# An mLSTM and MLP kernel: late gates on 128 partitions, and less work turned by TensorE

## The chip, the cores and the metric

The kernel runs on one core of one Trainium2 chip. A core has TensorE (matrix products), VectorE, ScalarE, GpSimd and SyncE, each with an instruction queue of its own that it works off in order, and 16 DMA engines. The metric is the device time of one execution in microseconds.

## What is computed

An mLSTM layer (4 batches, 8 heads, 768 time steps, head size 40) is followed by a gated MLP on its 3072 rows of 320 features. Per batch and head, over time t:

```python
m_new = np.maximum(f[t] + m, i[t])
f_stab, i_stab, m = np.exp(f[t] + m - m_new), np.exp(i[t] - m_new), m_new
C = f_stab * C + i_stab * outer(v[t], k[t])
n = f_stab * n + i_stab * k[t]
y[t] = sigmoid(o[t]) * (C @ q[t]) / max(abs(n @ q[t]), 1)
# then, for all rows x of y: 
h = x @ w_in            # 320 -> 2048
out = (h * sigmoid(h)) @ w_out
```

## The kernel before

Time is cut into 12 pieces of 64 steps. A *unit* is one piece for two of the four batches, so there are 24; unit n has piece n // 2. A unit multiplies scores (keys with queries), weighs them by the gates (tile D), adds up its own values ("near", from D) and the values of the running state ("far", from qt, the queries times lq), divides, and gives x: 128 rows of 320 features. It also adds to the state Cm.

Three units make a *step* of the MLP, so there are 8. `Step.mm1` (line 849) makes ph, the hidden layer, for one of 16 feature chunks of 128, `Step.act` (856 to 880) the gate product g, `Step.mm2` (901) the output. TensorE alternates between the first product of chunk fc and the second of chunk fc - 2, and the loop over steps j and chunks fc (from `for j in range(NSTEP)`) puts between them what the next three units need. In step 0 the units 3, 4 and 5 are done at chunks 5, 9 and 12 (`PLACES`): `block` (scores of the next unit, near and far values, state), `close` (weighing, line 576, and norm), `level`, `scale`, `carry` (the state, lines 747 and 757). The PSUM pool `psH` has two buffers, which ph and half of a unit's state use in turn.

The order on every engine is the order in which the code is written; no scheduler changes it. The table `FILL`, chunk by chunk, says what else is done in step 0: `wmake(n)` makes the next n weight parts (two ScalarE passes, lines 280 and 281, then VectorE, 282, into wi, wo or wtc) and issues the load of a later part on SP's queue; `halve` splits a wtc part into wh (303, 305). So weights, gates and units share VectorE and ScalarE in step 0. In the steps 1 to 7 the weights are there.

The **gates** come from two inputs of 32 rows (batch and head) by 768 columns (time), side by side in the tile `home` as f, i, m, LF and a pattern. `gates(lo, hi)` (167 to 185) scans m, then forms the exponents and scans LF within each piece, all on 32 partitions. Columns 0 to 255 are done early; `late` does 256 to 767 in two halves of 256 in the chunks 3 to 12. `spread` writes LF of two pieces to DRAM (LFd), from where units load it as D and lq, and turns the gate sums i into aT (time on the partitions) with three TensorE transposes (line 200) and two VectorE copies (207). `spread_far` does the other eight pieces: two VectorE block transposes (228) and ScalarE copies (233).

The **x** of a unit has to be turned, features on the partitions. `xpose` (794) does that with three TensorE transposes into PSUM. For the units in `AROUND` (6 to 23 without 8) `turn_out` instead transposes blocks of 32 on VectorE (766) and stores them to DRAM with four DMAs (768), and `turn_in` loads them back (776). `xput` then splits x into xh (ScalarE, 805) and xl (VectorE, 806).

The **state** of a unit (`state`) is 16 matmuls in 64x64 tiles into two PSUM banks for units from 3 on (line 705), and for units 0 to 2 eight matmuls over all 128 rows into one bank (717), added by `carry` at line 759.

Of the kernel before, what the change touches and what calls it, by code (L numbers as in the profile page):

```python
# [8 lines left out]
F32 = mybir.dt.float32  # L9
# [5 lines left out]
ALU = mybir.AluOpType  # L15
# [4 lines left out]
L = 64  # L20
# [23 lines left out]
def mlstm_mlp_kernel(  # L44
# [6 lines left out]
    fg: bass.AP,  # L51
    w_in: bass.AP,
# [54 lines left out]
    LFd = dr.tile([NC, BH, L], F32, name="LFd")  # L107
# [80 lines left out]
    def spread(lo, hi, eng):  # L188

        c0, c1 = lo // L, hi // L  # L190
        eng.dma_start(
            LFd[c0:c1].rearrange("c r t -> r c t"),
            LF[:, lo:hi].rearrange("r (c t) -> r c t", t=L),
        )
        yield
        pt = psU.tile([128, 512], F32, tag="u", name=f"pt{lo}")

        for c in range(c0 - 1, c1):
            w = slice(c * L, (c + 2 - (c == NC - 1)) * L)
            nc.tensor.transpose(  # L200
                pt[: w.stop - w.start, c * BH : (c + 1) * BH], i_t[:, w], ident[:BH, :BH]
            )
            if (c - c0) % 3 == 1:
                yield
        for k in range(2):
            r = slice(k * L, (k + 1) * L)
            nc.vector.tensor_copy(  # L207
                aT[r, c0:c1, :, :],
                pt[r, (c0 - k) * BH : (c1 - k) * BH].rearrange(
                    "p (c q d h) -> p c q d h", q=NP, d=2, h=H  # L210
                )[:, :, :, k, :],
            )
        yield


    def spread_far(lo, hi, eng):

        c0, c1 = lo // L, hi // L
        eng.dma_start(
            LFd[c0:c1].rearrange("c r t -> r c t"),  # L220
            LF[:, lo:hi].rearrange("r (c t) -> r c t", t=L),
        )
        yield
        n = (c1 - c0) * BH
        src = i_t[:, lo:hi].rearrange("r (c b x) -> r b c x", b=2, x=32)
        at = home[:BH, : 2 * n].rearrange("x (b c r) -> x b c r", b=2, r=BH)
        for b in range(2):
            nc.vector.transpose(at[:, b], src[:, b])
            yield
        for k in range(2):  # L230
            for b in range(2):
                r = k * L + b * 32
                nc.scalar.copy(
                    aT[r : r + 32, c0:c1].rearrange("p c q h -> p (c q) h"),
                    at[:, b].rearrange("x c (q d h) -> x (c q) d h", q=NP, d=2)[:, :, k, :],
                )
            yield
# [132 lines left out]
    for t in Cm:  # L370
        nc.gpsimd.memset(t, 0.0)

# [10 lines left out]
    class Unit:  # L383
# [66 lines left out]
        def load_d(self):  # L450
            n, c, p = self.n, self.c, self.p
            self.Dm = p3.tile([128, H, L], F32, tag="D", name=f"D{n}")
            for k in range(2):
                r = p * 2 * H + k * H
                nc.sync.dma_start(
                    self.Dm[k * L : (k + 1) * L],
                    LFd[c, r : r + H, :].unsqueeze(0).broadcast_to([L, H, L]),
                )
# [28 lines left out]
        def load_q(self):  # L487
            n, c, p = self.n, self.c, self.p
            if c > 0:
                self.lq = p2.tile([128, H, L], F32, tag="lq", name=f"lq{n}")  # L490
                lf = LFd[c, p * 2 * H : (p + 1) * 2 * H, :].rearrange(
# [200 lines left out]
        def state(self):  # L692
# [3 lines left out]
            if n >= UPS:  # L696
                self.pu = [
                    pool_.tile([128, 4, D1], F32, tag=tag, name=f"pu{n}_{tag}")
                    for pool_, tag in ((psU, "u"), (psH, "h"))
# [35 lines left out]
        def carry(self, copy=nc.scalar.copy, steps=(0, 1)):  # L735
# [4 lines left out]
            for a in range(2):  # L740
# [14 lines left out]
                for d in range(2) if n >= UPS else ():  # L755
                    w = v[:, d * 4 : (d + 1) * 4]
                    nc.vector.tensor_tensor(out=w, in0=w, in1=pu[d][r], op=ALU.add)
                if n < UPS:
                    nc.vector.tensor_tensor(out=v, in0=v, in1=pu[r], op=ALU.add)
# [170 lines left out]
    AROUND = set(range(2 * UPS, NU)) - {3 * UPS - 1}  # L930
# [33 lines left out]
    def run(n, it):  # L964
        for _ in range(n):
            next(it, None)
# [31 lines left out]
    for _ in range(2):  # L998
# [4 lines left out]
    near, far = spread(2 * L, 4 * L, nc.gpsimd), spread_far(4 * L, S, nc.gpsimd)  # L1003
    late = [gates(4 * L, 8 * L), gates(8 * L, S)]
# [81 lines left out]
        1: lambda: (wmake(1), u3.expo_act(), u3.keep(), u3.near(), u4.load_qk()),  # L1086
# [13 lines left out]
        3: lambda: (wmake(1), u4.add(), run(1, late[0])),  # L1100
        4: lambda: (wmake(1), u4.exp(), run(1, late[0])),
        5: lambda: wmake(1),
        6: lambda: (halve(4), wmake(2), run(1, late[0])),
        7: lambda: (wmake(1), run(2, late[0])),
        8: lambda: (wmake(1), run(1, late[1])),
        9: lambda: wmake(2),
        10: lambda: (halve(6), wmake(1), run(2, late[1])),
        11: lambda: (wmake(1), run(1, late[1])),
        12: lambda: (wmake(1), run(2, late[1])),
        13: lambda: (wmake(1), run(2, far)),  # L1110
        14: lambda: (units[8].load(), run(1, far)),
        15: lambda: run(3, far),
# [22 lines left out]
    for j in range(NSTEP):  # L1135
        st = steps[j]
        for fc in range(NFC):
# [36 lines left out]
            if 6 in at and at[6].n in AROUND:  # L1174
                at[6].xput(steps[j + 1])
# [9 lines left out]
def _layout(inputs):  # L1185
# [15 lines left out]
    for w, x in enumerate((q, k)):  # L1201
# [21 lines left out]
        "fg": gate(inputs["f_gate"]),  # L1223
        "w_in": bits(w_in[:256]),
# [33 lines left out]
```

## Time and profile before

| | us |
|---|---|
| three runs | 430.94, 431.71, 431.79 |
| their median | 431.71 |
| the profiled execution | 431.02 |
| its span, first to last instruction | 429.2 |

| engine | busy us | share of the span | instructions |
|---|---|---|---|
| TensorE, matmuls | 422.4 | 98% | 5062 |
| TensorE, weight loads | 391.7 | 91% | 5062 |
| VectorE | 288.5 | 67% | 650 |
| ScalarE | 220.6 | 51% | 481 |
| GpSimd | 124.8 | 29% | 135 |

The profile shows one execution of the program. "Start" is us from the span's start. PE is TensorE, PEld its weight loads, DVE VectorE, ACT ScalarE, POOL GpSimd, SP SyncE, SPq its DMA queue. Matmuls overlap, so what one costs is read from the start of the next group. A row such as `th<-ph` names the tile that is written and the one that is read; brackets give the idle time before it and what ended it. The granted clock of TensorE is 1.0 of full speed over the whole span. Step 0 goes from 19.9 to 78.6 us. A row of busy time by stretch gives the stretch and its length, then for PE, PEld, DVE, ACT and POOL the busy us and the number of instructions, the granted clock, the share of time that the 16 DMA engines were busy, and GB/s.

### The profile page before, as it was taken

How to read it: one execution, taken by the hardware profiler on the slowest of the kernel's cores; microseconds unless marked ns; L12 is line 12 of the kernel's file. 1: busy time of each engine (PE TensorE's matmuls, PEld its weight loads, DVE VectorE, ACT ScalarE, POOL GpSimd, SP SyncE). 2: the span in 40 equal slices, each digit the busy share in tenths (PEclk: the TensorE clock that was granted, in tenths of full speed). 3: DMA queues.
4: the chain of work that ended last, by engine and by line, in shares of the span. 5: the costliest groups of instructions: out<-in, count | busy, mean ns of one | idle time of the engine just before them, and what ended most of it. 6: DMA issues, size and time to landing. Idle time of an engine off the chain costs nothing.

```text
span 429.2 us, 12518 instructions
## 1 busy us (share of the span) xinstructions
PE 422.4 (98%) x5062; PEld 391.7 (91%) x5062; DVE 288.5 (67%) x650; ACT 220.6 (51%) x481; POOL 124.8 (29%) x135
## 2 busy tenths in 40 slices
PE   8999999999999999999999999999999999999995
PEld 4767677899999999999999999999999999999995
DVE  5888799877887677467765677566764756443342
ACT  7684866755755454454454644444454543353331
POOL 5734135234234423043412344034320400000000
PEclk9999999999999999999999999999999999999999
DMA  8999696334551775127660575316750231001001
GB/s 272 387 366 311 177 299 165 117 89 141 159 169 21 196 196 155 31 61 189 174 172 2 123 218 139 118 25 179 209 163 22 54 94 20 18 9 39 2 2 46
DMA packets 62650, 57.17 MB, mean 133 GB/s; under 512 B 31440, under 2 KB 49184, under 8 KB 62592
## 3 DMA queue, kind: packets, MB, share of 16 engines
q1 hardware_dynamic: 62288, 55.94, 45.7%
q8 instruction: 40, 0.66, 0.7%
q10 hardware_dynamic: 208, 0.26, 0.2%
q0 software_dynamic: 96, 0.16, 0.1%
q14 instruction: 18, 0.15, 0.1%
HBM read 48.99 MB, written 7.36 MB: 131 GB/s over the span
## 4 chain that ended last, share of the span: by engine, by line
PE 80%; issue 17%; DVE 1%; ACT 1%; POOL 0%; POOLq 0%; ACTq 0%; DVEq 0%
PE ph L849 35%; PE pout L901 33%; PE p L549 3%; PE p L637 2%; PE p L620 2%; PE dummy L999 1%; PE pu_u L705 1%; PE pu_h L705 1%; DVE D L576 0%; PE e L396 0%; PE px L794 0%; PE pu L717 0%; PE po L604 0%; PE p L794 0%; POOL qt L533 0%
## 5 line engine op out<-in xcount | busy, mean ns | idle before, releaser
L856 ACT ACTIVATE th<-ph 128x384 f32<-128x384 f32 x128 | 62.4, 488 | 106.7 <-PE ph L849 106.2
L849 PE MATMUL ph<-xh,wh 128*128 128x384 f32 x336 | 113.8, 339 | 0.0
L849 PE MATMUL ph<-xl,wh 128*128 128x384 f32 x336 | 113.6, 338 | 0.0
L901 PE MATMUL pout<-woh,gh 128*128 128x320 f32 x336 | 105.5, 314 | 0.0
L901 PE MATMUL pout<-woh,gl 128*128 128x320 f32 x336 | 103.9, 309 | 0.0
L901 PE MATMUL pout<-wol,gh 128*128 128x320 f32 x336 | 103.3, 307 | 0.0
L876 ACT CAST gh<-th 128x384 fp32r<-128x384 f32 x112 | 57.5, 513 | 81.3 <-DVE th L871 69.9
L880 DVE TENSOR_TENSOR gl<-th,gh 128x384 fp32r<-128x384 f32 x112 | 64.6, 577 | 47.5 <-ACT gh L876 47.5
L871 DVE SCALAR_TENSOR_TENSOR th<-th,ph 128x384 f32<-128x384 f32 x112 | 61.4, 548 | 51.1 <-ACT th L856 50.6
L849 PE MATMUL ph<-xh,wl 128*128 128x384 f32 x224 | 75.9, 339 | 0.0
L747 POOL TENSOR_TENSOR Cm<-Cm,lq 40x328 f32<-40x328 f32 x40 | 30.6, 764 | 114.6 <-PE p L637 111.8
L901 PEld LDWEIGHTS pout<-woh,gh 128*128 128x128 f32 x336 | 63.0, 188 | 0.9
L849 PEld LDWEIGHTS ph<-xh,wh 128*128 128x128 f32 x336 | 63.1, 188 | 0.2
L849 PEld LDWEIGHTS ph<-xl,wh 128*128 128x128 f32 x336 | 63.0, 188 | 0.2
L901 PEld LDWEIGHTS pout<-woh,gl 128*128 128x128 f32 x336 | 63.0, 188 | 0.1
L901 PEld LDWEIGHTS pout<-wol,gh 128*128 128x128 f32 x336 | 63.1, 188 | 0.0
L533 POOL TENSOR_TENSOR qt<-qk,lq 104x512 f32<-104x512 f32 x22 | 29.7, 1348 | 99.4 <-ACT lq L529 89.3
L849 PEld LDWEIGHTS ph<-xh,wl 128*128 128x128 f32 x224 | 42.1, 188 | 0.0
L901 PE MATMUL pout<-wo,g 128*128 128x320 f32 x96 | 28.7, 435 | 0.0
L516 POOL TENSOR_TENSOR D<-D,am 128x512 f32<-128x512 f32 x20 | 26.1, 1303 | 4.0 <-DMA D<-LFd 2.5
L508 POOL TENSOR_TENSOR am<-mask,aT 128x512 f32<-128x512 f32 x20 | 24.1, 1205 | 6.6 <-DVE aT L207 5.1
L576 DVE TENSOR_TENSOR D<-p,D 128x512 f32<-128x512 f32 x24 | 16.5, 689 | 13.7 <-PE p L637 12.3
(136 smaller groups left out, 524.4 us busy)
## 6 DMA issues: line engine op xcount, KB each, us to landing
qk<-in_qk_dram SPq DMA_DIRECT2D x24, 512.0 KB, 5.1
ko<-in_ko_dram SPq DMA_DIRECT2D x24, 320.0 KB, 5.3
wro<-in_w_out_dram SPq DMA_DIRECT2D x8, 640.0 KB, 7.3
D<-LFd SPq DMA_DIRECT2D x40, 128.0 KB, 3.1
lq<-LFd SPq DMA_DIRECT2D x40, 128.0 KB, 4.9
wri<-in_w_in_dram SPq DMA_DIRECT2D x8, 512.0 KB, 6.0
vb<-in_vp_dram SPq DMA_DIRECT2D x48, 82.0 KB, 5.1
out_dram<-ob SPq DMA_DIRECT2D x45, 80.0 KB, 2.1
```

The lines of the kernel that those rows point to most:

```text
L508: nc.gpsimd.tensor_tensor(out=self.am, in0=mask.unsqueeze(1).broadcast_to([128, H, L]), in1=aT[:, self.c, self.p, :].unsqueeze(2).broadcas ...
L516: nc.gpsimd.tensor_tensor(out=self.Dm, in0=self.Dm, in1=self.am, op=ALU.add)
L533: nc.gpsimd.tensor_tensor(out=self.qt, in0=self.q[:KS], in1=self.lq[:KS], op=ALU.mult)
L549: nc.tensor.matmul(self.ps[d * L : (d + 1) * L, a * 4 + j, :], self.k[r, d * 4 + j, :], self.q[r, d * 4 + j, :], start=True, stop=True,)
L576: nc.vector.tensor_tensor(out=self.Dm, in0=self.ps, in1=self.Dm, op=ALU.mult)
L747: nc.gpsimd.tensor_tensor(out=v, in0=v, in1=self.lq[r, :, L - 1].unsqueeze(2).broadcast_to([D, H, D1]), op=ALU.mult,)
L849: nc.tensor.matmul(ph, w, x, start=(i == 0), stop=(i == len(ops) - 1))
L856: nc.scalar.activation(th, ph, AF.Tanh, scale=0.5)
L871: nc.vector.scalar_tensor_tensor(out=th, in0=th, scalar=1.0, in1=ph, op0=ALU.add, op1=ALU.mult)
L876: nc.scalar.copy(gh, th)
L880: nc.vector.tensor_tensor(out=gl, in0=th, in1=gh.bitcast(F32), op=ALU.subtract)
L901: nc.tensor.matmul(self.po[t], g[:, ts], w, start=(fc == 0 and i == 0), stop=(last and i == len(ops) - 1),)
```

## The change

Five things, in the words of the diff. `late_load`, `late_gates`: after the two scans of m on 32 rows, the columns 256 to 767 are laid out as four blocks of 128 columns on 128 partitions. f and i of the blocks 1 to 3 come straight from DRAM (a new input lg, the same numbers in another layout), m by three DMAs within SBUF; the rest of the gate arithmetic runs once on 128 by 128, and three more DMAs bring i back to the 32 rows. LF goes to DRAM as LFl by one DMA of SP, where GpSimd's queue stored it before. `spread` now does for all pieces what `spread_far` did. The state of unit 2 goes to 64x64 tiles like that of later units, into the pools psU and psO. `AROUND` takes in the units 3 and 4, and their x is put four chunks behind their block instead of two. `FILL` moves the pieces of `near`, `late` and `far` to other chunks.

```diff
-    LFd = dr.tile([NC, BH, L], F32, name="LFd")
+    LFd = dr.tile([4, BH, L], F32, name="LFd")
+    LFl = dr.tile([2, 4, BH, L], F32, name="LFl")
+    chunk = lambda c: LFd[c] if c < 4 else LFl[c % 2, (c - 4) // 2]
...
-    def spread(lo, hi, eng):
+    LATE, LB = 4 * L, 128
+    NB = (S - LATE) // LB
+    lanes = lambda k, first=0: home[:, k * S + LATE - first : k * S + LATE + LB]
+    block_rows = lambda b: slice(b * BH, (b + 1) * BH)
+    block_cols = lambda b, first=0: slice(LATE + b * LB - first, LATE + (b + 1) * LB)
+
+    def late_load():
+
+        to = home[BH:, : 2 * S].rearrange("r (k s) -> r k s", k=2)[:, :, LATE : LATE + LB]
+        nc.sync.dma_start(to, lg)
+
+    def late_gates():
+
+        for lo in range(LATE, S, 4 * L):
+            hi = lo + 4 * L
+            nc.vector.tensor_tensor_scan(
+                m_t[:, lo:hi], f_t[:, lo:hi], i_t[:, lo:hi], m_t[:, lo - 1 : lo],
+                op0=ALU.add, op1=ALU.max,
+            )
+            yield
+        for b in range(1, NB):
+            nc.sync.dma_start(lanes(2, 1)[block_rows(b)], m_t[:, block_cols(b, 1)])
+        yield
+        f, i, m, lf, p = lanes(0), lanes(1), lanes(2, 1), lanes(3), lanes(4)
+        tt = nc.vector.tensor_tensor
+        tt(out=f, in0=f, in1=m[:, :LB], op=ALU.add)
+        tt(out=f, in0=f, in1=m[:, 1:], op=ALU.subtract)
+        nc.vector.tensor_scalar(f, f, -120.0, None, op0=ALU.max)
+        yield
+        nc.vector.tensor_tensor_scan(lf, p, f, 0.0, op0=ALU.mult, op1=ALU.add)
+        tt(out=i, in0=i, in1=m[:, 1:], op=ALU.subtract)
+        tt(out=i, in0=i, in1=lf, op=ALU.subtract)
+        yield
+        nc.sync.dma_start(
+            LFl.rearrange("c b r t -> (b r) c t"), lf.rearrange("r (c t) -> r c t", t=L)
+        )
+        for b in range(1, NB):
+            nc.sync.dma_start(i_t[:, block_cols(b)], i[block_rows(b)])
+        yield
+
+    def spread(lo, hi, eng=None):
...
-            if n >= UPS:
+            if n > 1:
                 self.pu = [
                     pool_.tile([128, 4, D1], F32, tag=tag, name=f"pu{n}_{tag}")
-                    for pool_, tag in ((psU, "u"), (psH, "h"))
+                    for pool_, tag in ((psU, "u"), (psH, "h") if n >= UPS else (psO, "o"))
                 ]
...
-                for d in range(2) if n >= UPS else ():
+                for d in range(2) if n > 1 else ():
                     w = v[:, d * 4 : (d + 1) * 4]
                     nc.vector.tensor_tensor(out=w, in0=w, in1=pu[d][r], op=ALU.add)
-                if n < UPS:
-                    nc.vector.tensor_tensor(out=v, in0=v, in1=pu[r], op=ALU.add)
...
-    AROUND = set(range(2 * UPS, NU)) - {3 * UPS - 1}
+    AROUND = set(range(UPS, NU)) - {2 * UPS - 1, 3 * UPS - 1}
...
-        1: lambda: (wmake(1), u3.expo_act(), u3.keep(), u3.near(), u4.load_qk()),
+        1: lambda: (run(2, near), wmake(1), u3.expo_act(), u3.keep(), u3.near(), u4.load_qk()),
...
-        3: lambda: (wmake(1), u4.add(), run(1, late[0])),
-        4: lambda: (wmake(1), u4.exp(), run(1, late[0])),
-        5: lambda: wmake(1),
-        6: lambda: (halve(4), wmake(2), run(1, late[0])),
-        7: lambda: (wmake(1), run(2, late[0])),
-        8: lambda: (wmake(1), run(1, late[1])),
-        9: lambda: wmake(2),
-        10: lambda: (halve(6), wmake(1), run(2, late[1])),
-        11: lambda: (wmake(1), run(1, late[1])),
-        12: lambda: (wmake(1), run(2, late[1])),
-        13: lambda: (wmake(1), run(2, far)),
+        3: lambda: (wmake(1), u4.add(), run(1, late), late_load()),
+        4: lambda: (wmake(1), u4.exp(), run(1, late)),
+        5: lambda: (run(1, late), wmake(1)),
+        6: lambda: (halve(4), wmake(2)),
+        7: lambda: (run(1, late), wmake(1)),
+        8: lambda: (wmake(1), run(1, late)),
+        9: lambda: (run(1, late), wmake(2)),
+        10: lambda: (halve(6), wmake(1)),
+        11: lambda: wmake(1),
+        12: lambda: (wmake(1), run(1, far)),
+        13: lambda: (wmake(1), run(1, far)),
         14: lambda: (units[8].load(), run(1, far)),
-        15: lambda: run(3, far),
+        15: lambda: run(2, far),
...
-            if 6 in at and at[6].n in AROUND:
-                at[6].xput(steps[j + 1])
+            there = at.get(6 if j > 0 else 4)
+            if there is not None and there.n in AROUND:
+                there.xput(steps[j + 1])
```

Three places where the order moves. First, SP's queue in the chunks 4 to 7 of step 0 (ko is unit 5's, wro chunk part 4's output weights, lq unit 5's, D unit 6's). Before:

```order
L475 DMA ko_710<-in_ko_dram 128x640
L261 DMA wro_808<-in_w_out_dram 128x2x640
L496 DMA lq_822<-LFd 64x2x256 x2
L261 DMA wrc_843<-in_w_tail_dram 128x512
L261 DMA wri_849<-in_w_in_dram 128x2x512
L261 DMA wro_874<-in_w_out_dram 128x2x640
L261 DMA wri_897<-in_w_in_dram 128x2x512
L455 DMA D_907<-LFd 64x512 x2
```

and with the change:

```order
L493 DMA ko_725<-in_ko_dram 128x640
L784 DMA xd_118<-xt_816 32x12x32 x4
L212 DMA home<-home 32x129 x3
L277 DMA wro_832<-in_w_out_dram 128x2x640
L514 DMA lq_846<-LFd 64x2x256 x2
L277 DMA wrc_862<-in_w_tail_dram 128x512
L277 DMA wri_868<-in_w_in_dram 128x2x512
L792 DMA px_887<-xd_118 128x3x128
L277 DMA wro_896<-in_w_out_dram 128x2x640
L277 DMA wri_916<-in_w_in_dram 128x2x512
L473 DMA D_928<-LFd 64x512 x2
```

Unit 3's x (xd) and the three copies of m now stand ahead of the load wro, and the way back (px) ahead of the next two weight loads. Second, VectorE from the weights of chunk part 4 (wo) to the cast part of the tail weights (wtc); D is unit 5's, x and Cm are unit 4's. Before:

```order
L282 SCALAR_TENSOR_TENSOR wo_893<-wro_808 128x640
L167 SCALAR_TENSOR_TENSOR home<-home 32x256
L863 SCALAR_TENSOR_TENSOR g_9_984<-th_9_905,ph_9_900 128x384
L576 TENSOR_TENSOR D_703<-p_916,D_703 128x512
...
L757 TENSOR_TENSOR Cm_138<-Cm_138,pk_991 40x164
L282 SCALAR_TENSOR_TENSOR wtc_1008<-wrc_843 128x256
L282 SCALAR_TENSOR_TENSOR wi_1014<-wri_849 128x512
L863 SCALAR_TENSOR_TENSOR g_10_1027<-th_10_1025,ph_10_1020 128x384
L806 TENSOR_TENSOR xl_828<-p_916,xh_827 128x3x128
```

and with the change:

```order
L298 SCALAR_TENSOR_TENSOR wo_912<-wro_832 128x640
L220 SCALAR_TENSOR_TENSOR home<-home 128x128
L221 TENSOR_TENSOR home<-home 128x128
L222 TENSOR_TENSOR home<-home 128x128
L879 SCALAR_TENSOR_TENSOR g_9_1005<-th_9_926,ph_9_921 128x384
L594 TENSOR_TENSOR D_718<-p_937,D_718 128x512
...
L775 TENSOR_TENSOR Cm_139<-Cm_139,pk_1012 40x164
L782 STREAM_TRANSPOSE xt_1026<-x_1016 128x384
L822 TENSOR_TENSOR xl_852<-px_887,xh_851 128x3x128
L298 SCALAR_TENSOR_TENSOR wtc_1041<-wrc_862 128x256
L298 SCALAR_TENSOR_TENSOR wi_1047<-wri_868 128x512
L879 SCALAR_TENSOR_TENSOR g_10_1060<-th_10_1058,ph_10_1053 128x384
```

The block transpose of unit 4 and the xl of unit 3 now stand ahead of wtc, where before xl of unit 4 stood behind g of chunk 10. Third, ScalarE from the tanh of chunk 10 to that of chunk 11, with the cast of the tail weights that follows. Before:

```order
L856 ACTIVATE th_10_1025<-ph_10_1020 128x384
L805 CAST xh_827<-p_916 128x3x128
L303 CAST wh<-wtc_1008 64x256 x2
L280 ACTIVATE wro_874<-wro_874 128x640
L281 ACTIVATE wro_874<-wro_874 128x640
L856 ACTIVATE th_11_1059<-ph_11_1054 128x384
```

and with the change:

```order
L872 ACTIVATE th_10_1058<-ph_10_1053 128x384
L319 CAST wh<-wtc_1041 64x256 x2
L296 ACTIVATE wro_896<-wro_896 128x640
L297 ACTIVATE wro_896<-wro_896 128x640
L872 ACTIVATE th_11_1084<-ph_11_1079 128x384
```

The cast of unit 4's x, which read TensorE's transposes (p), no longer stands between the tanh and the cast of wtc.

## Rows read from the trace of the kernel before

**Rows 1.** Busy time by stretch: step 0, whole.

```profile
19.90:78.60 58.70, 58.66 (x626) 41.17 (x625) 50.60 (x112) 41.73 (x85) 24.16 (x23) 1.00 0.85 265
```

**Rows 2.** Timeline of VectorE, chunk 1 (start us, us, engine, line, operation).

```profile
25.52 1.02 DVE L759 TENSOR_TENSOR Cm<-Cm,pu 40x328 f32<-40x328 f32 x2
...
27.20 0.55 DVE L863 SCALAR_TENSOR_TENSOR g<-th,ph 128x384 f32<-128x384 f32 x1
```

**Rows 3.** Timeline of TensorE: far values of unit 5.

```profile
66.09 0.44 PE L637 MATMUL p<-Cm,qt 40*64 40x41 f32 x16
```

**Rows 4.** Timeline of GpSimd: D of unit 6, qt of unit 5.

```profile
57.86 1.27 POOL L516 TENSOR_TENSOR D<-D,am 128x512 f32<-128x512 f32 x1
64.68 1.36 POOL L533 TENSOR_TENSOR qt<-qk,lq 104x512 f32<-104x512 f32 x1 [5.54 <-ACT lq L529]
```

**Rows 5.** Timeline of VectorE: carries of units 3 and 4, weighing of unit 5.

```profile
42.20 1.05 DVE L757 TENSOR_TENSOR Cm<-Cm,pk 40x164 f32<-40x164 f32 x1
...
55.68 0.67 DVE L576 TENSOR_TENSOR D<-p,D 128x512 f32<-128x512 f32 x1
...
58.40 0.92 DVE L757 TENSOR_TENSOR Cm<-Cm,pk 40x164 f32<-40x164 f32 x1
...
59.60 0.32 DVE L757 TENSOR_TENSOR Cm<-Cm,pk 40x164 f32<-40x164 f32 x1
59.96 0.43 DVE L282 SCALAR_TENSOR_TENSOR wtc<-wrc 128x256 uint32<-128x256 uint32 x1
```

**Rows 6.** Timeline of ScalarE, chunks 6, 8, 10 and 13.

```profile
44.19 0.48 ACT L805 CAST xh<-p 128x384 fp32r<-128x384 f32 x1 [1.45 <-PE p L794]
...
51.17 0.79 ACT L280 ACTIVATE wro<-wro 128x640 f32<-128x640 f32 x1
...
60.51 0.83 ACT L303 CAST wh<-wtc 64x256 fp32r<-64x256 f32 x2
...
70.60 0.49 ACT L856 ACTIVATE th<-ph 128x384 f32<-128x384 f32 x1 [1.54 <-PE ph L849]
```

**Rows 7.** Timeline of TensorE: states of units 2 and 3, transposes.

```profile
21.77 0.77 PE L717 MATMUL pu<-vb,kw 128*40 128x82 f32 x16
22.47 1.56 PE L849 MATMUL ph<-x,wi 128*128 128x384 f32 x4
...
28.18 0.37 PE L200 MATMUL pt<-ident,home 32*128 32x32 f32 x3
...
38.01 0.21 PE L705 MATMUL pu_u<-vb,kw 64*40 64x41 f32 x1
...
38.33 0.44 PE L637 MATMUL p<-Cm,qt 40*64 40x41 f32 x16
...
59.60 0.49 PE L794 MATMUL p<-ident,x 128*128 128x128 f32 x3
59.93 0.49 PE L849 MATMUL ph<-x,wi 128*128 128x384 f32 x1
```

**Rows 8.** View of the tile xt (count, least, median, most ns).

```profile
L766 DVE STREAM_TRANSPOSE xt<-x x17: 578/578/580, 91.5 to 360.1; 128x384 f32<-128x384 f32 x17
```

**Rows 9.** Timeline of SP's DMA queue, step 1: one unit's stores.

```profile
92.12 1.88 SPq L768 DMA_DIRECT2D xd<-xt  x4
```

**Rows 10.** Busy time by stretch: 46 to 48 us.

```profile
46.00:48.00 2.00, 1.99 (x8) 1.11 (x7) 0.86 (x2) 2.00 (x5) 0.00 (x0) 1.00 0.02 6
```

**Rows 11.** DMA issues, 47.3 to 47.8 us (last column: us to landing).

```profile
wri<-in_w_in_dram SPq DMA_DIRECT2D x1, 512.0 KB, 3.4
```

**Rows 12.** Timeline of VectorE: a gate scan of 128 columns.

```profile
3.88 0.41 DVE L167 TENSOR_TENSOR_SCAN home<-home 32x128 f32<-32x128 f32 x1 [3.88 <-DMA home<-in_ig_dram]
```

**Rows 13.** View of the tile xl, by way of DRAM and PSUM.

```profile
L806 DVE TENSOR_TENSOR xl<-px,xh x17: 548/1358/1367, 110.6 to 376.6; 128x384 fp32r<-128x384 f32 x17
L806 DVE TENSOR_TENSOR xl<-p,xh x4: 551/554/558, 44.7 to 126.3; 128x384 fp32r<-128x384 f32 x4
```

**Rows 14.** View of the tile wro: its loads' time to landing.

```profile
DMA to landing us min/median/max: 4.8/7.3/8.2
```

More of the change, by code (lines that the diff above doesn't have):

```diff
@@ L51, in mlstm_mlp_kernel @@
     fg: bass.AP,
+    lg: bass.AP,
     w_in: bass.AP,
@@ L186, in gates @@
         yield
-    def spread(lo, hi, eng):
-        c0, c1 = lo // L, hi // L
[L191 to L201, printed above, removed]
-            )
[L203 to L213, printed above, removed]
@@ L216, in spread_far @@
[L216 to L223, printed above, removed]
+    LATE, LB = 4 * L, 128
[3 more added lines that the diff above has]
+    block_cols = lambda b, first=0: slice(LATE + b * LB - first, LATE + (b + 1) * LB)
@@ L224, in spread_far @@
+    def spread(lo, hi, eng=None):
+        c0, c1 = lo // L, hi // L
+        if eng is not None:
+            eng.dma_start(
+                LFd[c0:c1].rearrange("c r t -> r c t"),
+                LF[:, lo:hi].rearrange("r (c t) -> r c t", t=L),
+            )
+            yield
         n = (c1 - c0) * BH
@@ L371, in mlstm_mlp_kernel @@
         nc.gpsimd.memset(t, 0.0)
+    nc.gpsimd.memset(lanes(4), 1.0)
+    nc.gpsimd.memset(lanes(4).rearrange("r (c t) -> r c t", t=L)[:, :, 0:1], 0.0)
     def bank(n, pool_, tag, shape, name):
@@ L456, in load_d @@
                     self.Dm[k * L : (k + 1) * L],
-                    LFd[c, r : r + H, :].unsqueeze(0).broadcast_to([L, H, L]),
+                    chunk(c)[r : r + H, :].unsqueeze(0).broadcast_to([L, H, L]),
                 )
@@ L490, in load_q @@
                 self.lq = p2.tile([128, H, L], F32, tag="lq", name=f"lq{n}")
-                lf = LFd[c, p * 2 * H : (p + 1) * 2 * H, :].rearrange(
+                lf = chunk(c)[p * 2 * H : (p + 1) * 2 * H, :].rearrange(
                     "(d a e) t -> a d (e t)", d=2, a=2
@@ L1002, in mlstm_mlp_kernel @@
     two = gates(2 * L, 4 * L)
-    near, far = spread(2 * L, 4 * L, nc.gpsimd), spread_far(4 * L, S, nc.gpsimd)
-    late = [gates(4 * L, 8 * L), gates(8 * L, S)]
+    near, far, late = spread(2 * L, 4 * L, nc.gpsimd), spread(4 * L, S), late_gates()
     widen()
@@ L1223, in _layout @@
         "fg": gate(inputs["f_gate"]),
+        "lg": np.stack(
+            [gate(inputs[x])[:, 3 * S // 6 :].reshape(B * H, 3, 128) for x in ("f_gate", "i_gate")], 2
+        ).swapaxes(0, 1).reshape(3 * B * H, 2, 128),
         "w_in": bits(w_in[:256]),
```

## The prediction

> **What bounds the kernel now.** I looked first at the busy time by stretch. In the first of the eight MLP steps, "step 0", TensorE is busy for 58.66 of 58.70 us [rows 1], and all of the change's edits lie there. That row alone says that whatever TensorE no longer does is won. But VectorE and ScalarE are each busy for over two thirds of the same stretch, and the DMA engines for 0.85 of it [rows 1]. So I read on, engine by engine in order of time, and asked which other queue ends just before TensorE needs it. There are two such places. One is the gate product g of feature chunk 1, which VectorE ends at 27.20 + 0.55 = 27.75 us [rows 2]; chunk 3's first matmul goes into the PSUM buffer that g frees, and TensorE comes to it at about 28.5. The other is the far half of unit 5's values, which started at 66.09 right after GpSimd ended qt at 64.68 + 1.36 = 66.04 [rows 3, 4]. That qt hangs on a long chain in two in-order queues: VectorE makes wtc (59.96), ScalarE casts it (60.51), then does chunk 5's output weights, a tanh, an exp and lq, and GpSimd multiplies [rows 4 to 6].
>
> **TensorE's own share.** The third unit's state took 22.47 - 21.77 = 0.70 us with 128-row matmuls; the same work in 64x64 tiles, as the later units do it, runs from 38.01 to 38.33, 0.32 us [rows 7]. That is 0.38 off. The three gate-sum transposes (pt) last 0.37, and the next matmul starts inside the last of them: 0.30 off. A unit's three x transposes hold TensorE from 59.60 to 59.93, 0.33, and they go for two units: 0.66 off [rows 7]. The sum is 1.34 us.
>
> **What is kept of it, first place.** By chunk 3 the first two edits have given 0.68, so TensorE would come to chunk 3 at 27.8 instead of 28.5. But g of chunk 1 ended at 27.75 already, and VectorE now has four state additions of 0.32 each in place of two that took 1.02 together [rows 2, 5]: 0.26 more, less where they overlap; I take 0.15. So chunk 3 starts at about 28.0, and 0.5 of the 0.68 is kept. VectorE's two small transposes of gate sums come after that g, and the two PSUM copies that they replace are gone: nothing.
>
> **Second place, step by step.** Unit 3's x now goes to DRAM and back. VectorE ended that unit's carry at 42.20 + 1.05 = 43.25 [rows 5]; half a microsecond earlier that is 42.75, and the added block transpose of 0.58 [rows 8] ends at 43.3. Only then can SP, whose queue is in order, issue the four stores: 1.88 us for four [rows 9], to 45.2. Three copies of m at the same pace follow, to 46.6, and only behind them the load of chunk 4's output weights ("wro"), which stood ahead of all this before. From 46 to 48 us the DMA engines were 0.02 busy, and the 512 KB that were issued then landed after 3.4 us [rows 10, 11]. For 640 KB I take 4.1, between 3.4 and 3.4 x 1.25 = 4.25: it lands at 50.7. ScalarE came to it at 51.17. It now comes sooner, since the cast of unit 3's x and the 1.45 us of waiting for TensorE ahead of it are gone [rows 6]: that cast ended at 44.67, and the work behind it now waits for VectorE's wtc alone, which comes right behind the transpose, at 43.3 + 0.43 = 43.75. So some 0.8 sooner, 50.35. So it waits 0.35 for the load.
>
> From there VectorE sets the pace. ScalarE's two passes (0.79 each, [rows 6]) end at 52.2, VectorE's own pass at 53.0. Then come the three late gate instructions on 128 columns (a scan of 0.41 as at the start [rows 12], and two subtractions that I put at 0.25 each): 53.9. Then g of chunk 9 (0.55), and the weighing of unit 5 starts at 54.4 instead of 55.68 [rows 5], 1.3 earlier: before, the late gates stood here with 256 columns at a time, and VectorE was the queue that was late. Now two instructions are added ahead of wtc: unit 4's block transpose, 0.58, and xl of unit 3, 0.55 [rows 8, 13]. What is left is 0.2. One more thing moves. In the carry of unit 4 one addition took 0.92 instead of 0.32, while GpSimd's addition to D ran (57.86 to 59.13) [rows 4, 5]. Unit 6's D is loaded behind more bytes than before, and VectorE comes 1.3 earlier, so that the two probably miss each other: up to 0.6 more. So wtc, and with it ScalarE's cast, qt and the far values, come 0.2 to 0.8 earlier. I take 0.6, nearer the upper end, since the D load waits for the landing of the late weights (eight DMAs of SP are in flight at most in this program, and each issue waits for the eighth before it).
>
> So at 66.09 the kernel gains **0.6 us**, while TensorE alone would have gained over a microsecond: it waits there about as long as it has saved. After that only unit 5's x is left, which still goes through TensorE; the chunk-6 weights, whose load also stands behind four stores and four copies, meet a ScalarE that waited 1.54 us for TensorE right behind them [rows 6]. I put that at nothing, and it costs if the load lands more than 2 us late. Steps 1 to 7 issue what they issued before.
>
> The profiled execution took 431.02 us, 429.2 of them in the span; the sum gives 431.02 - 0.6 = 430.4. The runs scatter: three others took 430.94, 431.71 and 431.79, median 431.71. The mean of the four is 431.4, and I forecast **430.8** from it; by the profiled one it would be 430.4, by the median 431.1. A change of less than 0.2%, 0.86 us, can't be told from none.
>
> **Rivals.**
> *TensorE is the bound throughout.* Then all 1.34 us are kept, and some tenths of waits around units 4 and 5 besides: 430.1, down to 429.7. For it: 58.66 of 58.70, and no long idle time of TensorE anywhere in step 0. Against it: qt ended 0.05 before the matmul that needs it. It wins if ScalarE's cast of wtc starts by 59.2.
>
> *The late load comes later* (the slower side). At chunk 8, ScalarE stands before chunk 4's weights, and VectorE's wo, g, weighing and wtc stand behind ScalarE. Each microsecond of delay goes through whole. The gain is used up at a landing time of 4.7 us, and at 5.6 the kernel is 0.86 slower. The landing times of these loads were 4.8 at least, 7.3 in the middle and 8.2 at most [rows 14]: by the middle one it would be 434. Against it: those loads were issued into full queues, and this one meets an empty one.
>
> *VectorE is held up by GpSimd.* xl of a unit took 0.548 us or 1.358, and two inputs in SBUF are what it has in the new path; the old one read x from PSUM and never took over 0.558 [rows 13]. If xl of unit 3 meets GpSimd's addition to D, 0.81 us more stand ahead of wtc, and the gain turns into -0.2: 431.6. For it: the carry's addition was held in the same place. Against it: the D load comes late, at about 58 to 60, and xl is due at 58.5. The Trainium skill has the rule on its page "SBUF — State Buffer", section "Who interferes with whom": a VectorE instruction with two SBUF inputs contends with a GpSimd instruction that reads SBUF, and whoever comes first holds the port to its end. The two values of xl agree with it; by that rule alone, with the two meeting, the sum would be the 431.6 above.
>
> **The numbers.** My forecast has 0.42, of which 0.07 gain over 0.86 us and the rest lie within 0.2%; its own range is 430.6 to 431.2. TensorE as the bound has 0.28, all faster. The late load has 0.17, of which 0.15 are slower. The port has 0.13, of which 0.11 are within the bound and 0.02 slower. Together: faster 0.35, same 0.48, slower 0.17. The range goes from the full TensorE gain on a fast run, 429.5, to a load that lands after 5.6 us, 432.3.
>
> **What would show it.** In the new profile: the state of unit 2 in 0.3 us; chunk 3 at 28.0; SP's load of wro behind xd at about 46.6, landing near 50.7; ScalarE waiting for a DMA before it, by some tenths; the weighing of unit 5 near 54.4; wtc near 59.3; far values of unit 5 released by qt on GpSimd, at 65.5, after an idle time of TensorE of over 1 us; from there the same pace as before. The forecast is wrong if TensorE never waits at unit 5 (first rival), if ScalarE waits over 1.5 us for wro (second), or if xl lasts 1.3 us (third).

## The result and the profile after

The changed kernel took 437.78 us (median of 6 runs, 436.56 to 440.53) where the kernel before took 431.75 (430.94 to 432.12): a ratio of 1.015, interval 1.011 to 1.019. Four more runs of it, on another occasion, gave 435.24, ratio 1.0085 (1.0064 to 1.0107); the ten together have a median of 436.6. It is slower, and the range of 429.5 to 432.3 misses it. Three slow runs of the experiments, each over 1.5% above the fastest of its kernel (439.64 in e1, 437.61 in e6, 437.52 in e8), count in the medians further down and not in the ratios. The profiled execution took 436.68, with a span of 434.9 where the one before had 429.2.

Where do the 5.7 us go? I compared the start of each chunk's first product on TensorE in the two traces. Step 0 began 0.61 later (20.60 for 19.99) and step 1 began 4.64 later (83.25 for 78.61), so step 0 itself is 4.03 us longer: 62.65 us for 58.62. Another 1.0 is lost later, at two places in the steps 2 and 4 (0.64 and 0.44). TensorE's timeline in step 0 (start, us, engine, line, operation; the idle time before it and what ended it in brackets):

```profile
22.85 1.56 PE L865 MATMUL ph<-x,wi 128*128 128x384 f32 x4
...
24.60 1.45 PE L865 MATMUL ph<-x,wi 128*128 128x384 f32 x4
...
28.81 1.56 PE L865 MATMUL ph<-x,wi 128*128 128x384 f32 x4
...
44.10 1.45 PE L865 MATMUL ph<-x,wi 128*128 128x384 f32 x4
...
48.53 1.56 PE L865 MATMUL ph<-x,wi 128*128 128x384 f32 x4 [1.01 <-DVE wi L298]
...
55.50 1.88 PE L917 MATMUL pout<-wo,g 128*128 128x320 f32 x6
59.79 2.93 PE L865 MATMUL ph<-x,wi 128*128 128x384 f32 x4 [2.40 <-DVE g L879]
...
64.81 1.45 PE L865 MATMUL ph<-x,wi 128*128 128x384 f32 x4
...
70.76 0.42 PE L655 MATMUL p<-Cm,qt 40*64 40x41 f32 x16
```

There is a wait of 1.01 us before chunk 8, which VectorE's wi ended, and one of 2.40 before chunk 10 (59.79), which the gate product g of chunk 9 ended. Behind it the four matmuls of a first product take 2.93 us in place of 1.45. The far values of unit 5 start at 70.76, 4.67 after their old place [rows 3]. Busy time by stretch shows why those matmuls are slow (the third number from the right is the granted clock):

```profile
58.00:59.00 1.00, 0.00 (x0) 0.00 (x0) 0.97 (x2) 1.00 (x4) 0.80 (x1) 1.00 1.02 384
59.00:60.00 1.00, 0.21 (x1) 0.21 (x2) 1.00 (x3) 1.00 (x3) 0.00 (x0) 0.91 1.12 351
60.00:61.00 1.00, 1.00 (x2) 0.63 (x3) 0.88 (x4) 0.18 (x1) 0.00 (x0) 0.50 1.08 252
...
62.00:63.00 1.00, 1.00 (x4) 0.70 (x3) 0.97 (x6) 0.00 (x0) 0.00 (x0) 0.50 1.07 249
63.00:64.00 1.00, 1.00 (x5) 0.77 (x4) 0.97 (x4) 0.49 (x1) 0.00 (x0) 0.88 0.83 202
64.00:65.00 1.00, 1.00 (x5) 0.76 (x4) 1.00 (x3) 0.28 (x1) 0.33 (x1) 1.00 0.35 98
```

TensorE stands still, and from 60 to 63 us the granted clock is 0.50, the lower of its two levels (1.2 GHz); by 64 it is back at 1.00.

What is g of chunk 9 late for? First there is SP's queue, in which wro is the load of chunk part 4's output weights, and then ScalarE, which needs that load:

```profile
44.42 1.89 SPq L784 DMA_DIRECT2D xd<-xt  x4
46.36 1.87 SPq L212 DMA_DIRECT2D home<-home  x3
48.32 0.53 SPq L277 DMA_DIRECT2D wro<-in_w_out_dram  x1
48.95 1.29 SPq L514 DMA_DIRECT2D lq<-LFd  x2
50.37 0.51 SPq L277 DMA_DIRECT2D wrc<-in_w_tail_dram  x1
50.98 0.94 SPq L277 DMA_DIRECT2D wri<-in_w_in_dram  x1
```

```profile
51.88 0.48 ACT L872 ACTIVATE th<-ph 128x384 f32<-128x384 f32 x1
54.16 0.80 ACT L296 ACTIVATE wro<-wro 128x640 f32<-128x640 f32 x1 [1.79 <-DMA wro<-in_w_out_dram]
54.86 0.78 ACT L297 ACTIVATE wro<-wro 128x640 uint32<-128x640 uint8 x1
```

The load is issued at 48.32, behind the four stores of unit 3's x (1.89 us, as [rows 9]) and the three copies of m, and lands 5.8 us later. ScalarE, which began on it at 51.17 before [rows 6], waits 1.79 for it and begins at 54.16. Behind ScalarE stands VectorE, beside GpSimd:

```profile
55.67 1.40 DVE L298 SCALAR_TENSOR_TENSOR wo<-wro 128x640 uint32<-128x640 uint32 x1 [1.89 <-ACT wro L297]
57.00 0.96 DVE L220 TENSOR_TENSOR_SCAN home<-home 128x128 f32<-128x128 f32 x1
57.88 1.06 DVE L221 TENSOR_TENSOR home<-home 128x128 f32<-128x128 f32 x1
58.98 0.29 DVE L222 TENSOR_TENSOR home<-home 128x128 f32<-128x128 f32 x1
59.19 0.55 DVE L879 SCALAR_TENSOR_TENSOR g<-th,ph 128x384 f32<-128x384 f32 x1
59.65 0.68 DVE L594 TENSOR_TENSOR D<-p,D 128x512 f32<-128x512 f32 x1
```

```profile
55.65 2.03 POOL L765 TENSOR_TENSOR Cm<-Cm,lq 40x328 f32<-40x328 f32 x2 [3.42 <-PE p L655]
57.76 1.04 POOL L526 TENSOR_TENSOR am<-mask,aT 128x512 f32<-128x512 f32 x1
...
68.90 1.29 POOL L551 TENSOR_TENSOR qt<-qk,lq 104x512 f32<-104x512 f32 x1 [2.47 <-ACT lq L547]
```

From wo to the end of the second subtraction VectorE needs 3.6 us. While GpSimd multiplies Cm and makes am, wo takes 1.40, the scan 0.96 and one subtraction 1.06; the other subtraction, next to nothing on GpSimd, takes 0.29. The weighing of unit 5 starts at 59.65 for 55.68 [rows 5], and qt of unit 5 at 68.90 for 64.68 [rows 4].

The smaller wait, before chunk 8, has the same pattern. VectorE's wtc, which took 0.42 in the kernel before, takes 1.31 beside GpSimd's addition to D, and ScalarE's cast and wi come after it:

```profile
44.32 1.31 DVE L298 SCALAR_TENSOR_TENSOR wtc<-wrc 128x256 uint32<-128x256 uint32 x1
```

```profile
44.08 1.27 POOL L534 TENSOR_TENSOR D<-D,am 128x512 f32<-128x512 f32 x1 [1.79 <-DMA D<-LFd]
```

So it is plain where the time goes; which of these links makes it, the experiments must tell.

### The profile page after: what moved, and what is told of

Read it like the earlier page. It is cut to its first block, busy times and chain, and to the rows that moved or that the text cites. A ratio compares the mean times of both kernels' runs of the same rounds, so it can differ in the third digit from the quotient of the medians.

```text
span 434.9 us, 12565 instructions
## 1 busy us (share of the span) xinstructions
PE 423.4 (97%) x5069; PEld 391.4 (90%) x5069; DVE 289.7 (67%) x648; ACT 220.9 (51%) x485; POOL 125.0 (29%) x136
## 4 chain that ended last, share of the span: by engine, by line
PE 68%; issue 17%; DMA 9%; DVE 2%; SPq 2%; ACT 1%; POOL 1%; POOLq 0%; ACTq 0%
PE ph L865 31%; PE pout L917 29%; DMA wro<-in_w_out_dram 3%; PE p L567 3%; PE p L655 2%; DMA wri<-in_w_in_dram 2%; PE p L638 2%; DMA vb<-in_vp_dram 2%; DMA D<-LFd 2%; PE pu_u L723 1%; PE pu_h L723 0%; SPq L212 0%; SPq L784 0%; DVE wo L298 0%; POOL qt L551 0%
## 5 line engine op out<-in xcount | busy, mean ns | idle before, releaser
L551 POOL TENSOR_TENSOR qt<-qk,lq 104x512 f32<-104x512 f32 x22 | 28.8, 1308 | 94.5 <-ACT lq L547 59.9
L865 PE MATMUL ph<-x,wi 128*128 128x384 f32 x64 | 25.1, 517 | 3.6 <-DVE g L879 2.4
```

What stands on the lines that cost most here:

```text
L551: nc.gpsimd.tensor_tensor(out=self.qt, in0=self.q[:KS], in1=self.lq[:KS], op=ALU.mult)
L865: nc.tensor.matmul(ph, w, x, start=(i == 0), stop=(i == len(ops) - 1))
```

## The experiments

Times are the medians; "step 0" is the time from the first product of step 0 to that of step 1 in the run's own trace (before: 78.61 - 19.99 = 58.62). The ratio is to runs of the kernel before that were taken along with each experiment. Step 0 leaves out the start-up, which differs from trace to trace by more than most of the effects (last section). A trace is one run: those of e10 (439.25) and e0 (435.81) are the longest of their four, those of e2 (430.50) and e3 (430.75) the shortest of their ten; the others lie between.

| kernel | us (runs) | ratio to before, interval | step 0, us |
|---|---|---|---|
| changed kernel | 437.78 (6) | 1.015, 1.011 to 1.019 | 62.65 |
| the same again (e0) | 435.24 (4) | 1.0085, 1.0064 to 1.0107 | 61.88 |
| e1 load wro first | 434.41 (10) | 1.0036, 1.0008 to 1.0065 | 59.79 |
| e2 TensorE turns units 3, 4 | 431.26 (10) | 0.9982, 0.9968 to 0.9997 | 58.00 |
| e3 before, units 3, 4 through DRAM | 432.85 (10) | 1.0018, 0.9998 to 1.0037 | 58.87 |
| e4 matmuls of zeros before chunk 9 | 435.02 (8) | 1.0067, 1.0042 to 1.0093 | 60.60 |
| e5 matmuls of zeros before chunk 10 | 437.28 (4) | 1.0128, 1.0103 to 1.0154 | 62.66 |
| e6 units 3, 4 turned last | 432.88 (10) | 1.0024, 1.0001 to 1.0048 | 57.95 |
| e8 as e6, loads first | 431.77 (12) | 1.0009, 0.9988 to 1.0030 | 58.12 |
| e9 as e2, loads first | 430.80 (12) | 0.9986, 0.9975 to 0.9998 | 58.43 |
| e10 late gates ahead of wo | 436.29 (4) | 1.0126, 1.0095 to 1.0156 | 62.72 |

**The place of the load.** In e1 the load of wro is issued ahead of unit 3's stores; nothing else moves.

```diff
+                if at[0].n == UPS:
+                    wload(1)
                 if at[0].n in AROUND:
                     at[0].turn_out()
...
-        5: lambda: (run(1, late), wmake(1)),
+        5: lambda: (run(1, late), wmake(1, False)),
```

> The changed kernel with one DMA moved: the load of chunk part 4's output weights (wro) is issued before unit 3's four stores xd and the three copies of m, not behind them. Theory A (the late load sets the end): in the changed kernel TensorE lost 2.57 us before chunk 9 to the chain wro landing 54.1, ScalarE, VectorE, and 1.72 us more to the lower clock behind that wait. With the load early, ScalarE starts on it at 52.4, g of the chunk before comes at about 56.4, chunk 9 starts at about 57.2 and the clock stays: 437.8 - 4.3 = 433.5. Rival B (VectorE's instructions, lengthened while GpSimd works, set the end): with wo 1.40, scan 0.96, subtraction 1.06 as measured, g comes at 58.2, TensorE still waits about 1 us: 435 with the clock kept, 436.5 without.

The wait before chunk 10 is gone, the clock stays, and step 0 is 2.86 us shorter: the place of the load is where the largest part comes from. VectorE's block is back to its lengths (wo 0.82, scan 0.42, subtractions 0.27 and 0.75), since it now ends, but for the last, before GpSimd begins; so e1 takes away the late load and the contention together, and 434.41 lies between theory A's 433.5 and rival B's 435. It is still slower than before, and two waits are left. The first comes again from a VectorE instruction beside GpSimd's addition to D, this time the carry's last addition (1.38 for 0.32). The second is at unit 5's far values: VectorE comes to wtc only at 62.53 (59.96 before, [rows 5]; this run's step 0 began 1.25 later), behind the block transpose and xl, and from its cast on ScalarE works without a break until lq, on which qt hangs:

```profile
49.52 1.56 PE L866 MATMUL ph<-x,wi 128*128 128x384 f32 x4 [1.13 <-DVE wi L298]
...
68.52 0.44 PE L656 MATMUL p<-Cm,qt 40*64 40x41 f32 x16 [0.93 <-POOL qt L552]
```

```profile
62.98 0.83 ACT L319 CAST wh<-wtc 64x256 fp32r<-64x256 f32 x2 [2.09 <-DVE wtc L298]
```

**The two parts apart.** e2 is the changed kernel without the way through DRAM for the units 3 and 4, e3 is the kernel before with that way alone.

```diff
-    AROUND = set(range(UPS, NU)) - {2 * UPS - 1, 3 * UPS - 1}
+    AROUND = set(range(2 * UPS, NU)) - {3 * UPS - 1}
```

(e2; in e3 the same line the other way round, and the x put four chunks behind the block.)

> The changed kernel with units 3 and 4 turned by TensorE again (AROUND as before); late gates, unit 2's state and the block transposes of gate sums stay. Theory A: the wro load then stands behind the three copies of m alone, issued near 42.4, landing near 47.5, and nothing waits for it: 433.5 plus the 0.66 of TensorE's transposes, less part of the 1.0 us wait at chunk 8 (wtc has no block transpose ahead of it): 433.2 to 434.2. If all of the loss comes with the way through DRAM, 431.4 or less. If it comes with the late gates, 437 or more.

> The kernel before with one part of the change alone: units 3 and 4 go through DRAM, put four chunks behind their block; gates as before. Theory A: wro stands behind four stores, issued near 46, landing 50 to 52, when ScalarE wants it at about 51 to 52: the loss is small, 0 to 1 us against before, 431.5 to 432.7. If the three copies of m don't matter and the stores alone make the load late: 434 or more, with the clock's fall.

Each part alone is within 0.2% of before: the late gates with unit 2's state gain 0.18%, the way through DRAM loses 0.18% (its interval touches none). e2 is the case in which all of the loss comes with the way through DRAM; e3 shows that this way alone doesn't make it. In e2 the wro load is issued at 41.52 behind the three copies, in e3 at 45.73 behind the four stores; nothing waits for either. Only both together, 3.8 us of SP's queue, make it late.

**The clock.** e4 and e5 add matmuls of zeros to the output sums, to keep TensorE at work.

```diff
+            if (j, fc) == (0, 9):
+                hum(16, st)
...
+        for k in range(n):
+            nc.tensor.matmul(st.po[k % UPS], identb, m, start=False, stop=False)
```

(e4; `m` is a tile of zeros, 128x320, which GpSimd clears at the start; in e5 the first line has chunk 10.)

> The changed kernel with 16 short matmuls of zeros (about 2.1 us) added to the output sums just before chunk 9's first product, so that TensorE works while it waits for VectorE; the sums are unchanged. If the lower clock of 59.8 to 63.4 comes from the idle time before it, chunk 9 starts as late as now (59.8) but takes 1.45 instead of 2.93 us for its first four matmuls, and the time is 437.8 - 1.7 = 436.1. If the clock falls for another reason, 437.8.

> The changed kernel with 16 matmuls of zeros (about 2.2 us, added to the output sums) where TensorE really waited: before chunk 10's first product. In the run before, they stood one chunk too early. If the lower clock follows from the idle time, the start of chunk 10 stays where it is (59.8, give or take the start-up's 0.6), its first four matmuls take 1.45 us in place of 2.93, and the time is 1.7 us under the changed kernel's. If the clock falls all the same, no difference.

e4 was set wrong: TensorE waits before chunk 10, not 9, and so I said 59.8 of the wrong product (the text of e1 names chunk 9 too). What it showed instead is worth more. TensorE was given 2.2 us more to do between the chunks 8 and 9 and began chunk 9 1.45 us later in step 0 than in the first profile, and yet step 0 came out 1.3 to 2.0 us shorter than in the two profiles of the changed kernel. (The times alone don't show that gain: the interval of e4's ratio overlaps that of e0.) VectorE and GpSimd show why:

```profile
55.87 0.82 DVE L298 SCALAR_TENSOR_TENSOR wo<-wro 128x640 uint32<-128x640 uint32 x1 [2.54 <-ACT wro L297]
56.61 0.42 DVE L220 TENSOR_TENSOR_SCAN home<-home 128x128 f32<-128x128 f32 x1
56.94 0.27 DVE L221 TENSOR_TENSOR home<-home 128x128 f32<-128x128 f32 x1
57.24 0.29 DVE L222 TENSOR_TENSOR home<-home 128x128 f32<-128x128 f32 x1
```

```profile
57.37 1.58 POOL L765 TENSOR_TENSOR Cm<-Cm,lq 40x328 f32<-40x328 f32 x2 [5.59 <-PE p L655]
```

The load was no earlier (ScalarE waited for it until 54.36), and wo still began at 55.87; but GpSimd's multiplication of Cm, which waits for unit 4 on TensorE, now began at 57.37, when VectorE was nearly through. The four instructions took 1.7 us in place of 3.6. So the contention of the two engines lengthens this block by about 1.9 us, apart from the load.

e5 kept the clock at 1.00 and saved what was expected at its place: chunk 10's first four matmuls took 1.56 us, and chunk 11 began at 62.86 in place of 64.81. But step 0 is as long as it was, 62.66 us for 62.65:

```profile
59.50 1.56 PE L865 MATMUL ph<-x,wi 128*128 128x384 f32 x4 [0.18 <-DVE g L879]
...
62.86 1.45 PE L865 MATMUL ph<-x,wi 128*128 128x384 f32 x4
...
71.03 0.44 PE L655 MATMUL p<-Cm,qt 40*64 40x41 f32 x16 [1.33 <-POOL qt L551]
```

The time saved was given back in full: TensorE waited 0.44 us for g before chunk 12 and 1.33 for qt at unit 5's far values. My 1.7 us were wrong: at unit 5 TensorE, fast or slow, comes at about the time of the next thing that it needs. By how much it is early or late depends on the run. In e5 the chain to qt was itself held up, since wtc ran beside GpSimd's addition to D and took 1.50 for 0.42. In the second profile (e0) xl was held in the same way, and there TensorE waited for qt even behind the slow stretch:

```profile
63.98 1.50 DVE L298 SCALAR_TENSOR_TENSOR wtc<-wrc 128x256 uint32<-128x256 uint32 x1
```

```profile
70.96 0.44 PE L655 MATMUL p<-Cm,qt 40*64 40x41 f32 x16 [0.31 <-POOL qt L551]
```

The first row is of e5, the second of e0. In the first profile neither was held; qt ended at 70.19 and TensorE came at 70.76, so there the slow clock can have cost up to 0.57 us.

**The changed kernel again.**

> The changed kernel once more, unaltered, for a second profile and more times on the chip of the next two runs. The first six times lay between 436.56 and 440.53. If the wait before chunk 10 and the lower clock behind it are its rule, the same again: 436 to 441, with a TensorE wait of 2 us or more before chunk 10 and a stretch at half the clock. If they were the accident of one profiled run, the new trace shows neither and the loss stands elsewhere.

It has the wait before chunk 10 again, 2.23 us, and the clock at 0.50 from 60 to 63. The wait of 1.01 before chunk 8 is not there, since wtc came just behind GpSimd's addition to D and took 0.38 where the first profile has 1.31, beside it. That one comes and goes (0.43 in e4, 0.46 in e5, none in e10); the late load is there in all five traces that have SP's queue unchanged.

**VectorE's order.** In e10 the late gates' second part stands ahead of wo, where VectorE only waits.

```diff
-        8: lambda: (wmake(1), run(1, late)),
+        8: lambda: (run(1, late), wmake(1)),
```

> The changed kernel with one swap on VectorE: in chunk 8 the scan and the two subtractions of the late gates stand before wo, not behind it. The load stays as late as it is (landing near 54.1). VectorE was idle for 1.1 to 1.9 us before wo, and behind it GpSimd's work on Cm and am (55.5 to 58.8) lengthened scan and subtractions from 1.0 to 2.3 us. If that queue behind the load is what the time goes through, g of chunk 9 comes 2 us sooner and the kernel gains 2 us, with the load no earlier. If only the load's landing counts, 0.5 us or less.

Half of it came true, but not in the time. With the load still late (ScalarE waited for it until 52.98, which is 1.2 us earlier than in the first profile) the wait before chunk 10 vanished, and chunk 10 started at 56.17. It was all given back at unit 5:

```profile
68.10 0.66 PE L655 MATMUL p<-Cm,qt 40*64 40x41 f32 x16 [2.21 <-POOL qt L551]
```

```profile
63.39 1.75 POOL L534 TENSOR_TENSOR D<-D,am 128x512 f32<-128x512 f32 x1 [5.51 <-DMA D<-LFd]
66.76 1.28 POOL L551 TENSOR_TENSOR qt<-qk,lq 104x512 f32<-104x512 f32 x1 [1.62 <-ACT lq L547]
```

Unit 6's D, whose load also stood behind the stores and copies on SP, came to GpSimd at 63.39 for 57.86 [rows 4]. Of these 5.5 us the issue makes 2.2 (53.79 for 51.62); the rest is the way from issue to GpSimd, 9.6 us where before it was 6.2 at most. ScalarE takes the exponent of that D ahead of unit 5's lq, and so qt was late all the same. TensorE waited 2.21 us there, and from 68 to 74 its granted clock was 0.50 (the three runs without a trace, 435.53 to 436.48, are no shorter than the changed kernel's second four). The late loads are a train: take the first out of the way, and the next one sets the end.

**All of it at once.** e6 writes the turning of the units 3 and 4 behind the chunk's other work, on VectorE and on SP. e8 also puts the weight loads ahead of the gates' copies, and e9 does that to e2.

```diff
-                if at[0].n in AROUND:
+                if j > 0 and at[0].n in AROUND:
                     at[0].turn_out()
...
                 FILL[fc]()
+                if 0 in at and at[0].n in AROUND:
+                    at[0].turn_out()
...
-        5: lambda: (run(1, late), wmake(1)),
+        5: lambda: (wmake(1), run(1, late)),
...
-        9: lambda: (run(1, late), wmake(2)),
+        9: lambda: (wmake(2), run(1, late)),
```

(The first two pieces are e6, all four e8, the last two on top of e2 are e9.)

> The changed kernel with the block transposes of units 3 and 4 and their stores written behind the fill of their chunk. On VectorE wtc then comes ahead of xt; on SP the three copies of m and the wro load come ahead of the four stores. Theory A (place in the queues alone): wtc starts at 43.8, before GpSimd's addition to D at 44.1, and lasts 0.43; the 1.0 us wait at chunk 8 goes; wro is issued near 42.4, lands by 48, and the wait before chunk 10 goes; ahead of unit 5's far values wtc comes 0.6 us sooner than it would. TensorE's savings are then kept: 0.66 below the kernel with TensorE's transposes (431.26), 430.6. Rival B (the way through DRAM costs in itself, by more traffic and longer VectorE instructions): 432.5 to 434.

> The kernel of e6 with the weight loads also ahead of the gates' own DMAs: in the chunks 5 and 9 the load of wro comes first, then the copies of m (or of LF and i), then unit 3's (4's) stores. Theory: e6 still scatters since its wro load, issued at 44.5 behind three copies of m, has little to spare. Now it is issued near 41, lands by 48, and TensorE's whole saving is kept in most runs: 430.6, with no run over 433. Rival (the way through DRAM itself makes the scatter): about e6's 432.9 again.

> The kernel of e2 (units 3 and 4 turned by TensorE) with the same order, load before the copies. In e2 nothing waited for that load, so no difference from it: 431.2, 0.3 to 0.6 above e8 if TensorE's transposes are worth their 0.66.

In the traces of e6 and e8 the loss is gone (in e6 wro is issued at 44.46, wtc takes 0.42), and step 0 is shorter than before by 0.7 and 0.5, no more than two traces of one kernel can differ. The times don't follow: those of e6 go from 430.73 to 434.53, with one at 437.61, those of e8 from 430.24 to 434.92, with one at 437.52, while e9, which differs from e8 only in that TensorE turns the units 3 and 4, stays between 430.11 and 431.62. So each theory had a part of it: the place in the queues makes the large loss, and with the way through DRAM the times scatter more. In e8 ScalarE waits 0.55 for unit 6's D, on which unit 5's qt hangs, and which in e9 was there 2.7 us sooner (GpSimd ended it at 60.14, in e8 at 62.83). But the far values of unit 5 began at 65.80 without a wait in the profile, so this trace lost next to nothing there. It lost its time elsewhere: step 0 is 0.5 shorter than before, and the run still took 432.19 for 431.02, since TensorE fell 1.5 us behind at one place in step 2, before the last matmul of a unit's far values:

```profile
159.90 0.25 PE L655 MATMUL p<-Cm,qt 40*64 40x41 f32 x1 [1.25 <-issue]
```

"issue" means that TensorE waited for nothing that the profile shows. The same matmul waits 0.40 us in the first profile of the changed kernel, 0.39 in e1, 0.44 in e6 and 1.74 in e10. The three other traces with late gates and the way through DRAM (e0, e4, e5) don't have it, and neither have before, e2, e3 and e9. Whether it makes the long runs was not seen, since neither trace of e6 and e8 is of a long run; what it is, and what makes the scatter, stays open. **e9 and e2 alone came out below the kernel before**: e9 by 0.14% (0.02 to 0.25), 430.80 against 431.39, and e2 by 0.18% (0.03 to 0.32). Both intervals only just leave out no gain, and both gains lie within the 0.2% that the prediction set as its bound.

## Why the prediction was wrong, step by step

- *TensorE's own share* was nearly right. Unit 2's state took 0.44 instead of 0.70 (22.41 to 22.85), 0.26 off where I had 0.38; pt's 0.30 went, and the x of unit 3 gave 0.32 (shift before chunk 7). That of unit 4 can't be read at the half clock; in e6 it gave 0.33.
- *First place*: forecast 0.5 kept by chunk 3; measured 0.28 (the lag fell from 0.61 to 0.33), 0.35 in e2. The floor was not the one named: g of chunk 1 ended at 28.54, but chunk 3 followed right behind unit 3's scores at 28.81, with no wait in the profile. What was not kept stands ahead of the scores, in the second product of chunk 0, whose start was followed by the scores after 1.94 us instead of 1.71 (1.95 in e2). What held it up there is open. The share was a little too large.
- *Second place, SP's queue*: "to 46.6, and only behind them the load". The order was right; it was 48.32. Of the 1.7 us, 1.1 are xt, which ended at 44.40 instead of 43.3 (I had counted VectorE half a microsecond early, and this run began 0.6 late), and 0.5 the three copies, which took 1.87 where I had 1.4.
- **The step that failed**: "For 640 KB I take 4.1 ... it lands at 50.7 ... So it waits 0.35 for the load." It landed 5.8 us after its issue. Six runs in which this load was issued between 45.7 and 49.1 had 4.8 to 6.5, and e6, which issued it at 44.46, had 4.5; none came down to 4.1. So of the 3.4 us by which it landed later than forecast, 1.7 are the landing time and 1.7 the late issue of the point above. I had taken the time of a load that met idle engines and had nothing behind it, though the rows of all such loads said 4.8 at least [rows 14]. "This one meets an empty one" looked only at what is ahead in the queue. Two loads of lq, wrc and wri follow within 3 us, and from 50 us on the DMA engines were full, where before the load had been under way since 36.83. That what follows lengthens it was not tried. Busy time by stretch of the changed kernel, DMA share the last but one:

```profile
48.00:50.00 2.00, 1.47 (x5) 0.94 (x6) 1.35 (x3) 2.00 (x5) 0.00 (x0) 1.00 0.26 54
50.00:64.00 14.00, 11.60 (x158) 8.02 (x157) 11.78 (x26) 7.45 (x16) 4.29 (x4) 0.88 1.02 302
```

- *The rival that came true* is the late load, at 0.17. Its price was worked out well as far as it went: each microsecond goes through whole. Landing at 54.1 instead of 50.7 makes 3.4 us, less the 0.6 of gain 2.8 slower, 434.2. The next step (1.9) and the 1.0 us after step 0 make up the rest to the profiled 436.68, with some to spare.
- *VectorE behind the load*: I counted wo, scan and subtractions as 0.8, 0.41 and two of 0.25. Late as they were, they ran beside GpSimd's work on unit 4: 1.40, 0.96 and 1.06, together 1.9 more, and e4 took it away without moving the load. I had the mechanism as a rival, but looked for it at xl alone. xl of unit 3 took 0.52 in the changed kernel and 1.53 in the second profile of it. The Trainium skill has the rule in "SBUF — State Buffer", section "Who interferes with whom": a VectorE instruction with two SBUF inputs contends with a GpSimd instruction that reads SBUF. All three instructions have two, and the traces agree: 1.40, 0.96 and 1.06 us beside GpSimd, 0.82, 0.42 and 0.27 without it in e4.
- *What was to show it*: ScalarE waited 1.79 us for wro, over the 1.5 that I had named for the second rival; xl was not at fault in the first profile. The other sign misled: TensorE did not wait at unit 5, which I had named as the sign of the first rival, because it had already waited 2.40 us before chunk 10.
- *TensorE as the bound throughout*, the rival with 0.28, is out: it waited 1.01 and 2.40 us in step 0.
- *Not foreseen*: the clock's fall, which cost little in the end, 0.57 us at most in the first profile and nothing in e0.
- *After step 0* I expected no difference. The first profile lost 1.0 us in the steps 2 and 4, where TensorE waited for nothing that the profile shows. Five of the eight traces with both parts of the change have such a wait at the same matmul of step 2, 0.39 to 1.74 us, the traces of e2, e3 and e9 none. What it is stays open.

## What to carry to other kernels

Before adding transfers to an in-order DMA queue, list what stands behind them, with the time at which each is wanted; two additions that cost next to nothing alone (here 0.2% or less) can make the work behind them late together. Price a load by the slowest of its kind in the trace, not by one that met an empty queue, and look at what is issued right behind it. When one queue falls behind, its work meets other partners: check which VectorE instructions with two SBUF inputs now run beside GpSimd, and keep such work, and the reserve of the chains that are nearly critical, ahead of the wait and not behind it.

## What the runs showed that was not expected

TensorE's clock fell to 0.50 behind waits of 2.23 and 2.40 us (and 2.21 in e10) and stayed there for some 3.4 us (6.8 in e10, worked out from the shares of 0.50 in each row); waits of 1.01 and 1.33 us were followed by no fall. In e10 there is a second fall, for 3.4 us from 166.6 on, behind the wait of 1.74 us in step 2, while e8's 1.25 at the same matmul was followed by none.

VectorE's CAST of 32x256 at the very start took 0.31 where it began at 6.39 (before) and 0.85 where it began at 5.99 (changed), beside GpSimd's memset of Cm (5.33 to 6.57); a clamp of 128x128 (L218) took 0.23 alone and 1.34 beside qt. Both have one SBUF input, so it is not only instructions with two that took longer beside GpSimd.

The start-up scatters by 2 us over the twelve traces (step 0 began at 19.48 to 21.59) with code that is nearly the same. ScalarE's wait for unit 2's ko is one source, ending at 15.81 before, at 16.60 and 17.59 in the two profiles of the changed kernel. The length of step 0 leaves that out and so shows effects that the times hide. But the two profiles of the changed kernel differ by 0.77 us in it, so a smaller difference between two traces (as among e2, e6, e8 and e9) shows nothing by itself.
